# Scores by row halves of the array, one PSUM ring, one transposing DMA for q and k, masks on the vector engine

## The chip, the cores and the metric

The kernel runs on one core of one Trainium2 chip. A core has engines that run side by side: TensorE (matrix products, PE in the profile; its weight loads are PEld), VectorE (DVE), ScalarE (ACT), GpSimd (POOL) and SyncE (SP), and 16 DMA engines that they share. GpSimd and SyncE issue the transfers of this kernel. The metric is the device time of one execution in microseconds.

## The reference, cut to what matters

Four sequences of 768 positions with eight heads of 64: attention with a local window of 96 and eight global positions, a distance bias per head, then a two-layer network with a squared ReLU on all 3072 rows.

```python
scores = scale * np.matmul(q, k.transpose(0, 1, 3, 2))        # q, k, v: (4, 8, 768, 64)
rel = pos[:, None] - pos[None, :]
is_global = pos[None, :] < n_global                           # 8
is_local = (rel >= 0) & (rel < n_local)                       # 96
dist = np.where(is_global & ~is_local, float(n_local), np.abs(rel))
scores = scores - slopes[:, None, None] * dist                # one slope per head
scores = np.where(is_global | is_local, scores, -1e9)
a = softmax(scores)
x = np.matmul(a, v)                                           # then (3072, 512)
r = np.maximum(x @ w_in, 0.0)                                 # w_in (512, 2048)
out = (r * r) @ w_out                                         # w_out (2048, 512)
```

## The kernel before, in words

The 3072 rows are 24 tiles of 128; each sequence has six. A tile's queries look at the keys of their own tile and of the tile before (the eight global keys of the sequence are copied into columns of that one which the window doesn't reach). The first tile of a sequence has its own keys alone. Two tiles make a block of the network; there are 12 blocks, and w_in and w_out are cut into eight steps.

*A tile's way.* GpSimd loads q, k and v with a cast to bf16 (`swdge`, line 186; tile 0's q and k come from SyncE in fp32, line 194). For tiles below `JQK` = 10 TensorE transposes q and k (`emit_tr`, line 375), and ACT or DVE copies the transposes out (`any_copy`, lines 297 and 299). q goes to `qz`, where each pair of heads has two blocks of 128 rows: the first with the even head in rows 0 to 63 and zeros below, the second with the odd head in rows 64 to 127 and zeros above. From tile 10 on SyncE transposes with two DMAs (`emit_dT`, lines 414 and 418); q is then loaded by two DMAs into `qpad`, which holds the zeros already. One product of 128 rows by 256 columns gives the scores of two heads for one block of keys (`emit_sc`, line 442). A tile has eight of these, two in each of four PSUM tiles `sc`; the first tile of a sequence has four. ACT takes exp (line 482), DVE multiplies by the mask factors `E` (line 503). For tiles 0 to 2 (`NBIAS`) the mask is added on TensorE instead, by products of `sid` and `pb` (line 451). `po` (line 549) is the product with v, which has a column of ones per head for the sum; DVE divides (lines 574 and 575) to `x`. x is transposed by TensorE (line 611) for tiles below `JX` = 10 and by a SyncE DMA (line 635) from there on.

*The network.* For each block and step, `hT` (line 659) is eight products of 256 columns, ACT applies ReLU (line 680), DVE squares (line 692), and `acc` (line 723) takes four products of 512 columns, two per tile. After eight steps a tile's acc is copied out (297 or 299) and stored by SyncE (line 768).

*PSUM* has eight banks: two for acc, three shared by hT and the transposes, two for sc, one for po. q and k have ten load buffers each; v of all tiles has its own.

*Order.* `Plan` (lines 23 to 94) puts every operation on an engine: a list scheduler with hand-set costs, lags and landing times, which takes at each step the operation that can start first (then by `key`). The instructions of each engine run in this order; a wait holds up all that stands behind it. Scores of a tile run ahead of the block that needs them by about `LEAD` = 12 network steps, and its transposing DMAs wait for the transposed x of three tiles earlier.

*Start.* GpSimd makes the identity, issues q and k of tile 1, makes the position mask `pb` in four steps (lines 248 to 254), then issues v of tiles 0 and 1, tile 2 and so on, with the weights between the tiles (lines 277 to 285). DVE clears `qz` and writes all 24 columns of ones (line 243).

Of the kernel before, what the change touches and what calls it, by code (L numbers as in the profile page):

```python
# [22 lines left out]
class Plan:  # L23
# [7 lines left out]

    LAG = {"PE": 0.25, "ACT": 0.15, "DVE": 0.12, "SP": 2.6, "POOLQ": 2.5, "DMA": 0.0}

# [16 lines left out]
    def run(self):  # L50
        rings = {}
        free = {e: 0.0 for e in self.LAG}
# [10 lines left out]
        while ready:  # L63
            best = None
            for o in ready:
                at = o["at"]
                if o["takes"]:
                    tag, bufs, users = o["takes"]
                    ring = rings.setdefault(tag, [])
                    if len(ring) >= bufs:  # L70
                        old = ring[-bufs]
                        if any("end" not in u for u in old):
                            continue
                        at = max([at] + [self.after(u, o["engines"]) for u in old])
                for e, cost in o["engines"].items():
                    r = (max(at, free[e]), o["key"], cost, o["n"])
                    if best is None or r < best[0]:
                        best = (r, o, e)
# [3 lines left out]
            o["start"], o["engine"], o["end"] = r[0], e, r[0] + o["engines"][e]  # L82
            free[e] = o["end"]
            if o["takes"]:
                rings[o["takes"][0]].append(o["takes"][2])
# [12 lines left out]
def kernel(  # L98
# [32 lines left out]
    NG = NBLK * NSTEP  # L131
    NACC = 2
    NPLAIN = 1
    NFIRST = 4
    NBIAS = 3
    JQK, JX = 10, 10
    NQ, NPAD, NKT, NQZ = 10, 8, 2 * TPB, 4
# [4 lines left out]
    ps_h = ctx.enter_context(tc.tile_pool(name="ps_h", bufs=5 - NACC, space=PSUM))  # L142
    ps_sc = ctx.enter_context(tc.tile_pool(name="ps_sc", bufs=2, space=PSUM))
    ps_o = ctx.enter_context(tc.tile_pool(name="ps_o", bufs=1, space=PSUM))
# [5 lines left out]
    q_ring = [const([P, d_model], BF16, f"q_{i}") for i in range(NQ)]  # L150
    q_pad = [const([P, NPAIR, 2, P], BF16, f"qpad_{i}") for i in range(NPAD)]
    k_ring = [const([P, d_model], BF16, f"k_{i}") for i in range(NQ)]
    v_sb = [const([P, H, D + 1], BF16, f"v_{j}") for j in range(NT)]
    kT = [const([P, NPAIR, P], BF16, f"kT_{i}") for i in range(NKT)]
    qz = [const([P, NPAIR, 2, P], BF16, f"qz_{i}") for i in range(NQZ)]
# [4 lines left out]
    E = const([P, NPAIR, 2, 2, P], BF16, "E")  # L160
    E0 = const([P, NPAIR, 2, P], BF16, "E0")
# [4 lines left out]
    zero = const([P, 4 * P], BF16, "zero")  # L166
    plan = Plan()
    NHS = 14
    E_AT = 14.0
    NWARM = 8  # L170
    HOLD = {}
# [4 lines left out]
    clock = [4.2]  # L176
# [8 lines left out]
    def swdge(name, dst, src, t):  # L185
        nc.gpsimd.dma_start(out=dst, in_=src)  # L186
        clock[0] += t
        land[name] = clock[0]

    q_tile, k_tile = {}, {}  # L190
    for j in range(NPLAIN):
        for n, src in (("q", q), ("k", k)):
            t_ = const([P, d_model], FP32, f"plain_{n}{j}")
            nc.sync.dma_start(
                out=t_.rearrange("p (h d) -> p h d", h=H),
                in_=src_rows(src, j).rearrange("h p d -> p h d"),
            )
            (q_tile if n == "q" else k_tile)[j] = t_
            land[n, j] = 4.1 + 2.1 * j + (1.05 if n == "k" else 0.0)


    def load_v(j):
        swdge(("v", j), v_sb[j][:, :, :D], src_rows(v, j).rearrange("h p d -> p h d"), 0.85)

    def load_qk(j):
        k_tile[j] = k_ring[j % NQ]
        todo = [("k", k_tile[j], k)]
        if j < JQK:
            q_tile[j] = q_ring[j % NQ]
            todo.insert(0, ("q", q_tile[j], q))  # L210
        else:
            q_tile[j] = q_pad[j % NPAD]
            s_ = src_rows(q, j).rearrange("(a e) p d -> e p a d", e=2)
            for e in range(2):
                swdge(("q", j), q_tile[j][:, :, e, e * D : (e + 1) * D], s_[e], 0.43)
        for n, dst, src in todo:
            swdge(
                (n, j), dst.rearrange("p (h d) -> p h d", h=H),
                src_rows(src, j).rearrange("h p d -> p h d"), 0.85,
            )  # L220

    def load_tile(j):
        load_qk(j)
        load_v(j)
# [17 lines left out]
    for j in range(NT):  # L242
        nc.vector.memset(v_sb[j][:, :, D : D + 1], 1.0)
    make_identity(nc, ident)
    load_qk(1)


    nc.gpsimd.iota(pbi, pattern=[[-P, 2], [-1, P]], base=0, channel_multiplier=1)
    nc.gpsimd.tensor_copy(pb, pbi)
    nc.gpsimd.affine_select(  # L250
        out=pb, in_=pb, compare_op=Alu.is_ge, fill=MASK_VAL,
        base=0, pattern=[[P, 2], [1, P]], channel_multiplier=-1,
    )
    nc.gpsimd.affine_select(
        out=pb, in_=pb, compare_op=Alu.is_ge, fill=MASK_VAL,
        base=n_local - 1, pattern=[[-P, 2], [-1, P]], channel_multiplier=1,
    )
    load_v(0)
    load_v(1)
    nc.vector.tensor_copy(ident32, ident)  # L260
    nc.vector.memset(qz[0].bitcast(I32), 0)
    nc.vector.memset(qz[1].bitcast(I32), 0)
    for h in range(H):
        nc.vector.tensor_scalar_mul(sid[h], ident, float(slopes[h] / scale))
    nc.vector.tensor_copy(pb0, pb[:, 0, :])
    nc.vector.tensor_scalar_max(
        pb0[:n_global, :], pb0[:n_global, :], float(-n_local)
    )
    nc.vector.memset(pb[:n_global, 1, :], float(-n_local))
    nc.vector.memset(qz[2].bitcast(I32), 0)  # L270
    nc.vector.memset(qz[3].bitcast(I32), 0)

    warm = ps_o.tile([P, 4 * P], FP32, name="warm", tag="po")
    for i in range(NWARM):
        nc.tensor.matmul(out=warm, lhsT=zero[:, :P], rhs=zero, start=True, stop=True)

    load_tile(2)
    load_w_in(0)
    load_tile(3)
    load_w_out(0)  # L280
    for w in range(1, NSTEP):
        load_w_in(w)
        load_w_out(w)
        if w in (3, 5):
            load_tile(NFIRST + (w - 3) // 2)
# [9 lines left out]
    def any_copy(e, dst, src):  # L295
        if e == "ACT":
            nc.scalar.copy(dst, src)  # L297
        else:
# [4 lines left out]
            ("E", pair), {"ACT": 0.65}, key=0.3 + pair, ready=E_AT,  # L303
            emit=lambda e, pair=pair: [
                nc.scalar.activation(
                    E[:, pair, :, h, :], pb, Act.Exp, scale=float(slopes[2 * pair + h])
                )
                for h in range(2)
            ],
        )  # L310
        for pair in range(NPAIR)
    ]

    def emit_E0(e, c):

        pairs = slice(2 * c, 2 * c + 2)
        nc.vector.tensor_copy(E0[:, pairs], E[:, pairs, 0])
        nc.vector.tensor_max(
            E0[:n_global, pairs], E[:n_global, pairs, 0], E[:n_global, pairs, 1]
        )  # L320
# [3 lines left out]
            ("E0", c), {"DVE": 0.6}, emit=lambda e, c=c: emit_E0(e, c), key=4 + c,  # L324
            deps=maskE[2 * c : 2 * c + 2],
        )
        for c in range(2)
# [3 lines left out]
    qz_users = [[] for _ in range(NQZ)]  # L331
    kT_users = [[] for _ in range(NKT)]
    qk_users = [[] for _ in range(NQ)]
    pad_users = [[] for _ in range(NPAD)]
# [5 lines left out]
    for j in range(NT):  # L340
# [3 lines left out]
        base = need - LEAD + 4 * (j % 2)  # L344


        if j in late:
            def emit_load(e, j=j):
                if j == JQK:
                    for i in range(NPAD):  # L350
                        nc.gpsimd.memset(q_pad[i].bitcast(I32), 0)
                load_tile(j)
            ld = plan.op(
                ("load", j), {"POOLQ": 2.6}, emit_load,
                deps=qk_users[j % NQ] + (pad_users[j % NPAD] if j >= JQK else []),
                key=base, ready=clock[0],
            )
            qk_users[j % NQ] = []
            if j >= JQK:
                pad_users[j % NPAD] = []  # L360
# [3 lines left out]
        zi, ki = j % NQZ, j % NKT  # L364
        fp = j < NPLAIN
        parts = []
        for n in ("q", "k") if j < JQK else ():
            users = []

            def emit_tr(e, j=j, n=n, fp=fp):  # L370
                pool, tag = ps_h, "hT"
                tr = pool.tile([P, NPAIR, P], FP32 if fp else BF16, name=f"tr{n}", tag=tag)
                src = (q_tile if n == "q" else k_tile)[j]
# [8 lines left out]
                ("tr", n, j), {"PE": 0.85 if fp else 0.24}, emit_tr,  # L382
                deps=[land[n, j]], key=base, ready=HOLD.get(j, 0.0),
                takes=("hT", 5 - NACC, users),
            )
            users.append(tr)
            if n == "q":
                for e_ in range(2):
                    half = slice(e_ * D, (e_ + 1) * D)

                    def emit_z(e, j=j, e_=e_, half=half, zi=zi):
                        any_copy(e, qz[zi][half, :, e_, :], tiles["tr", "q", j][half])

                    z = plan.op(
                        ("z", e_, j), {"DVE": 0.7 if fp else 0.43, "ACT": 0.57}, emit_z,
                        deps=[tr] + qz_users[zi], key=base + 0.1,
                    )
                    users.append(z)
                    parts.append(z)
            else:  # L400
                def emit_T(e, j=j, n=n, ki=ki):
                    any_copy(e, kT[ki], tiles["tr", n, j])

                c = plan.op(
# [412 lines left out]
```

The softmax here doesn't subtract the row's maximum and nothing guards it: scores larger than these inputs give would overflow.

## Time and profile before

| What | Value |
|---|---|
| Median of 8 runs | 225.87 us (225.43 to 226.69) |
| The profiled execution | 225.98 us |
| Its span, first to last instruction | 224.2 us |
| TensorE busy | 212.0 us (95%) |
| VectorE / ScalarE busy | 145.8 (65%) / 123.3 (55%) |
| DMA queue of GpSimd (loads) | 79,424 packets, 13.38 MB |
| DMA queue of SyncE (stores, transposes) | 35,696 packets, 14.16 MB |
| Mean granted TensorE clock | 0.991 |

The page's second part cuts the span into 40 slices of 5.6 us; a digit is a busy share in tenths. A line of the timeline gives start, duration, engine, line, operation, out<-in, shapes and count, and in brackets the idle time before it with what ended it. A product's duration holds the depth of the array, so the distance between starts, and not the duration, is what a product takes from the stream. A DMA row of GpSimd or SyncE is the time of issuing; how long the transfer takes to land is given apart.

### The profile page before, as it was taken

Reading aid. Unit: us, or ns where it says so; the run is one execution under the profiler, and the core shown is the slowest. Engines: PE = TensorE matmul, PEld = TensorE weight load, DVE = VectorE, ACT = ScalarE, POOL = GpSimd, SP = SyncE. Lnnn points to the kernel's source line nnn. Section 1 sums busy time; section 2 is a strip of 40 time slices with the busy share of each in tenths; the row PEclk is TensorE's granted clock in tenths of the full one; section 3 lists DMA queues with packets and bytes.
Section 4 is the critical chain, followed back from the end, with each engine's and each line's share of the span. In section 5 each row is a group of like instructions: output and inputs, shape, how many; then the busy total and the mean of one; then the engine's idle time right before and its main releaser. Section 6 shows DMA issues by size and latency. Waiting matters only on the chain.

```text
span 224.2 us, 4803 instructions
## 1 busy us (share of the span) xinstructions
PE 212.0 (95%) x1817; PEld 152.5 (68%) x1848; DVE 145.8 (65%) x380; ACT 123.3 (55%) x225; POOL 88.1 (39%) x118
## 2 busy tenths in 40 slices
PE   7399899999999999999999999999999999999992
PEld 3388567765777777776767767776776776776750
DVE  6466858676766768666666766867656856844530
ACT  2459666673755945645544744744645645643530
POOL 8996687699988975323705000000000000000000
PEclk9969999999999999999999999999999999999999
DMA  9999999999999999999997984166724430300202
GB/s 128 106 155 200 182 196 181 173 177 147 150 169 152 144 163 160 118 231 119 129 216 102 121 134 95 34 156 95 150 41 96 126 69 18 117 8 20 94 0 94
DMA packets 115142, 27.83 MB, mean 124 GB/s; under 512 B 105776, under 2 KB 112176, under 8 KB 115120
## 3 DMA queue, kind: packets, MB, share of 16 engines
q0 software_dynamic: 79424, 13.38, 80.4%
q1 hardware_dynamic: 35696, 14.16, 32.0%
q8 instruction: 14, 0.23, 0.4%
q14 instruction: 8, 0.07, 0.1%
HBM read 27.26 MB, written 6.29 MB: 150 GB/s over the span
## 4 chain that ended last, share of the span: by engine, by line
PE 81%; POOL 6%; DMA 4%; DVE 4%; ACT 2%; issue 1%; POOLq 0%
PE acc L723 35%; PE hT L659 35%; PE sc L442 7%; PE po L549 4%; DMA win<-in_moe_w_in_dram 4%; DVE hs L692 2%; POOL q L186 1%; POOL v L186 1%; POOL k L186 1%; ACT hr L680 1%; DVE o L299 1%; POOL win L186 1%; PE trx L611 1%; POOL wout L186 1%; ACT qz L297 1%
## 5 line engine op out<-in xcount | busy, mean ns | idle before, releaser
L659 PE MATMUL hT<-xT,win 128*128 128x256 bf16 x768 | 98.6, 273 | 1.1 <-DMA win<-in_moe_w_in_dram 0.7
L680 ACT ACTIVATE hr<-hT 128x512 f32<-128x512 f32 x96 | 57.3, 597 | 75.3 <-PE hT L659 73.3
L723 PE MATMUL acc<-wout,hs 128*128 128x512 bf16 x353 | 94.8, 379 | 1.6
L659 PEld LDWEIGHTS <-win 128*128 128x128 bf16 x768 | 74.6, 98 | 24.3 <-DMA win<-in_moe_w_in_dram 1.6
L692 DVE TENSOR_TENSOR hs<-hr 128x512 bf16<-128x512 f32 x96 | 66.0, 687 | 26.0 <-ACT hr L680 24.6
L723 PEld LDWEIGHTS <-hs 128*128 128x128 bf16 x384 | 34.5, 98 | 22.8
L482 ACT ACTIVATE esc<-sc 128x512 bf16<-128x512 f32 x78 | 46.2, 592 | 2.4 <-PE sc L442 2.3
L442 PE MATMUL sc<-qz,kT 128*128 128x256 bf16 x176 | 35.4, 277 | 0.5 <-DVE kT L299 0.3
L503 DVE TENSOR_TENSOR at<-esc,E 128x512 bf16<-128x512 bf16 x78 | 32.4, 416 | 0.1
L186 POOL DMA_DIRECT2D qpad<-in_q_dram x28 | 21.6, 803 | 23.6 <-DMA qz<-qpad 23.6
L186 POOL DMA_DIRECT2D v<-in_v_dram x24 | 22.0, 915 | 2.9 <-DVE at L503 2.1
L186 POOL DMA_DIRECT2D k<-in_k_dram x23 | 21.1, 919 | 2.9 <-PE sc L442 1.5
L575 DVE TENSOR_TENSOR x<-po,rs 128x256 bf16<-128x256 f32 x48 | 20.4, 424 | 1.7
L549 PEld LDWEIGHTS <-at 128*128 128x128 bf16 x352 | 17.2, 99 | 5.9
L574 DVE RECIPROCAL rs<-po 128x4 f32<-128x4 f32 x48 | 8.6, 180 | 18.5 <-PE po L549 17.9
L442 PEld LDWEIGHTS <-kT 128*128 128x128 bf16 x176 | 17.1, 99 | 3.4 <-DVE kT L299 0.8
L549 PE MATMUL po<-v,at 128*128 128x65 bf16 x352 | 18.9, 195 | 0.0
L299 DVE COPY o<-acc 128x512 f32<-128x512 f32 (+1 forms) x12 | 7.9, 662 | 8.2 <-PE acc L723 4.3
L297 ACT COPY o<-acc 128x512 f32<-128x512 f32 (+1 forms) x13 | 7.4, 570 | 5.3 <-PE acc L723 5.2
L522 DVE COPY kT<-kT 128x32 bf16<-128x32 bf16 x16 | 3.6, 226 | 9.2 <-PE sc L442 9.2
L297 ACT COPY qz<-trq 64x512 bf16<-64x512 bf16 x10 | 5.8, 580 | 6.5 <-DVE qz L299 4.7
L186 POOL DMA_DIRECT2D q<-in_q_dram x9 | 8.4, 930 | 1.5 <-DMA wout<-in_moe_w_out_dram 1.2
(52 smaller groups left out, 92.3 us busy)
## 6 DMA issues: line engine op xcount, KB each, us to landing
out_dram<-o SPq DMA_DIRECT2D x23, 256.0 KB, 2.5
v<-in_v_dram POOLq DMA_DIRECT2D x24, 128.0 KB, 6.7
k<-in_k_dram POOLq DMA_DIRECT2D x23, 128.0 KB, 6.4
win<-in_moe_w_in_dram POOLq DMA_DIRECT2D x8, 256.0 KB, 8.6
wout<-in_moe_w_out_dram POOLq DMA_DIRECT2D x8, 256.0 KB, 8.8
qpad<-in_q_dram POOLq DMA_DIRECT2D x28, 64.0 KB, 4.8
q<-in_q_dram POOLq DMA_DIRECT2D x9, 128.0 KB, 7.7
plain_q<-in_q_dram SPq DMA_DIRECT2D x1, 256.0 KB, 3.2
```

The lines of the kernel that those rows point to most:

```text
L186: nc.gpsimd.dma_start(out=dst, in_=src)
L297: nc.scalar.copy(dst, src)
L299: nc.vector.tensor_copy(dst, src)
L442: nc.tensor.matmul(out=sc[:, i, :, :], lhsT=kT[kj % NKT][:, p_, :], rhs=qz[zi][:, p_, :, :], start=True, stop=j >= NBIAS, skip_group_check ...
L482: nc.scalar.activation(out=esc, in_=sc.rearrange("p a b c -> p (a b c)"), func=Act.Exp, scale=scale,)
L503: nc.vector.tensor_mul(at, tiles.pop(("esc", j, pair)), bias.rearrange("p a b c -> p (a b c)"))
L549: nc.tensor.matmul(out=po[:, hi, :], lhsT=at[:, pair % 2 if first else i, h % 2, :], rhs=v_sb[kj][:, h, :], start=(i == 0), stop=(i == len ...
L575: nc.vector.tensor_tensor(out=x[:, 4 * hf : 4 * hf + 4, :], in0=po[:, :, :D], in1=rs.to_broadcast([P, 4, D]), op=Alu.mult,)
L659: nc.tensor.matmul(out=hT[:, c, :], lhsT=w_in_sb[s][:, kt, c * P : (c + 1) * P], rhs=tiles["xT", blk][:, kt, :], start=(kt == 0), stop=(kt ...
L680: nc.scalar.activation(hr, tiles.pop(("hT", blk, s)), Act.Relu)
L692: nc.vector.tensor_mul(hs, hr, hr)
L723: nc.tensor.matmul(out=tiles["acc", blk, sub], lhsT=hs[:, c, sub * P : (sub + 1) * P], rhs=w_out_sb[s][:, c, :], start=(s == 0 and c == 0) ...
```

## The change

- **Scores.** q and k of a tile stand transposed side by side in one buffer `qkT`, 64 rows per head: even heads in rows 0 to 63, odd heads in rows 64 to 127. A score product takes 64 rows and 128 columns of one head, odd and even in turn, into different banks. A tile gives four banks of [128, 4 x 128] (two for a first tile), keyed by odd/even and by group; from tile 4 on all 16 products of a tile are one operation that takes four banks at once (`takes` may now hold several).
- **PSUM.** Two banks for acc, six in one ring `g` for everything else.
- **Transposes.** `JQK` = `JX` = 6. From tile 6 on one DMA transposes q and k together. No zeros and no `qpad`. Six load buffers in place of ten.
- **Masks.** GpSimd only makes the positions; identities and `pb` are made on DVE. The tables `E` and `E0` are laid out by odd/even.
- **Ones.** Six tiles' columns of ones at the start, the other 18 later in DVE's stream, ahead of the loads of those tiles.
- **Loads.** q of tile 1, the positions, k of tile 1, v of 0 and 1, then the first step of w_in ahead of tile 2, and a written order of tiles and weights.
- **Planner.** A pull of 0.05 per unit of `key` (`URGE`), start times of the engines, and other costs.
- ACT runs one exp on a junk element at the start.

```diff
@@ class Plan @@
+    URGE = 0.05
                 for e, cost in o["engines"].items():
-                    r = (max(at, free[e]), o["key"], cost, o["n"])
+                    start = max(at, free[e])
+                    r = (start + self.URGE * o["key"], start, cost, o["n"])
...
@@ pools and buffers @@
-    JQK, JX = 10, 10
-    NQ, NPAD, NKT, NQZ = 10, 8, 2 * TPB, 4
+    JQK, JX = 6, 6
+    NQ, NKT = 6, 2 * TPB
+    NG = 8 - NACC
+    G = ("g", NG)
...
-    ps_h = ctx.enter_context(tc.tile_pool(name="ps_h", bufs=5 - NACC, space=PSUM))
-    ps_sc = ctx.enter_context(tc.tile_pool(name="ps_sc", bufs=2, space=PSUM))
-    ps_o = ctx.enter_context(tc.tile_pool(name="ps_o", bufs=1, space=PSUM))
+    ps_g = ctx.enter_context(tc.tile_pool(name="ps_g", bufs=NG, space=PSUM))
...
@@ start @@
-    for j in range(NT):
+    for j in range(NFIRST + 2):
         nc.vector.memset(v_sb[j][:, :, D : D + 1], 1.0)
-    make_identity(nc, ident)
-    load_qk(1)
+    load_part(0, 1)
     nc.gpsimd.iota(pbi, pattern=[[-P, 2], [-1, P]], base=0, channel_multiplier=1)
-    nc.gpsimd.tensor_copy(pb, pbi)
-    nc.gpsimd.affine_select(...)
-    nc.gpsimd.affine_select(...)
+    load_part(1, 1)
     load_v(0)
     load_v(1)
+    nc.scalar.activation(junk, zero[:, :1], Act.Exp)
...
+    nc.vector.tensor_scalar(ident32, pbi[:, 0, :], 0.0, None, op0=Alu.is_equal)
+    nc.vector.tensor_scalar(ident, pbi[:, 0, :], 0.0, None, op0=Alu.is_equal)
+    nc.vector.scalar_tensor_tensor(
+        out=pbt, in0=pbi, scalar=MASK_VAL, in1=pbi, op0=Alu.mult, op1=Alu.min
+    )
+    nc.vector.tensor_scalar(
+        pbw, pbi, float(n_local - 1), -MASK_VAL, op0=Alu.add, op1=Alu.mult
+    )
+    nc.vector.tensor_tensor(out=pb, in0=pbt, in1=pbw, op=Alu.min)
...
+    for w in "i0 T2 i1 T3 i2 o0 i3 o1 i4 o2 T4 i5 o3 i6 o4 T5 i7 o5 o6 o7".split():
+        kind, n = w[0], int(w[1:])
+        {"T": load_tile, "i": load_w_in, "o": load_w_out}[kind](n)
...
@@ tile loop @@
-                nc.sync.dma_start_transpose(
-                    out=qz[zi].rearrange("p a b c -> p (a b) c"),
-                    in_=q_tile[j].rearrange("p a b c -> p (a b c)"),
-                )
-                nc.sync.dma_start_transpose(out=kT[ki], in_=k_tile[j])
+                nc.sync.dma_start_transpose(
+                    out=T_.rearrange("p n a c -> p (n a) c"),
+                    in_=qk_ring[j % NQ].rearrange("p n c -> p (n c)"),
+                )
...
-                sc = ps_sc.tile([P, 2, 2, P], FP32, name="sc", tag="sc")
-                for i in range(2):
-                    p_, kj = (pair + i, j) if first else (pair, j - i)
-                    nc.tensor.matmul(
-                        out=sc[:, i, :, :],
-                        lhsT=kT[kj % NKT][:, p_, :],
-                        rhs=qz[zi][:, p_, :, :],
+            for g in gs:
+                for odd in range(2):
+                    sc[odd, g] = ps_g.tile([P, 4, P], FP32, name="sc", tag="g")
...
+            for g, pair, at, kt in todo:
+                for odd in range(2):
+                    half = slice(odd * D, (odd + 1) * D)
+                    nc.tensor.matmul(
+                        out=sc[odd, g][:, at, :],
+                        lhsT=qkT[(j - kt) % NKT][half, 1, pair, :],
+                        rhs=qkT[j % NKT][half, 0, pair, :],
...
+        for gs in [(0,), (1,)] if j < NSPLIT and not first else [tuple(range(groups))]:
+            n = 8 * len(gs)
+            o = plan.op(
+                ("sc", j, gs[0]), {"PE": 0.25 + 0.029 * n + (0.056 * n if j < NBIAS else 0)},
+                lambda e, gs=gs, f=emit_sc: f(e, gs), deps=deps, key=base + 1 + 2 * gs[0],
+                takes=(*G, busers[2 * gs[0] : 2 * gs[-1] + 2]),
+            )
```

## The prediction

> **What bounds the kernel now.** I read the page's busy rows first, then the TensorE timeline, then the SyncE and GpSimd issue timelines with the DMA landings. Row 2 of the page:
>
> ```profile
> PE   7399899999999999999999999999999999999992
> PEclk9969999999999999999999999999999999999999
> DMA  9999999999999999999997984166724430300202
> ```
>
> From the sixth slice (28 us) on TensorE is full; what it lacks is lost in the first slices, where the clock also drops once. The DMA engines are full up to slice 22 (123 us). So two stages have two limits: up to about 30 us loads arrive too late, after that the length of TensorE's stream decides. The stream's pitches come from starts in the timeline:
>
> ```profile
> 8.40 0.27 PE L451 MATMUL sc<-pb,sid 128*128 128x128 bf16 x2
> 11.26 0.40 PE L375 MATMUL trq<-ident,q 128*128 128x128 bf16 x4 [2.58 <-DMA q<-in_q_dram]
> ...
> 112.50 0.41 PE L549 MATMUL po<-v,at 128*128 128x65 bf16 x8
> 112.74 1.03 PE L723 MATMUL acc<-wout,hs 128*128 128x512 bf16 x4
> 113.60 1.04 PE L659 MATMUL hT<-xT,win 128*128 128x256 bf16 x8
> 114.48 0.38 PE L442 MATMUL sc<-qz,kT 128*128 128x256 bf16 x2
> 114.70 1.03 PE L723 MATMUL acc<-wout,hs 128*128 128x512 bf16 x3
> ```
>
> Start to start: eight po take 0.24 (0.030 each), four acc 0.86 (0.216), eight hT 0.88 (0.1094), two sc 0.22 (0.109). A four-block transpose takes 0.23, a 128-column bias product 0.055 (two in 0.11 at 8 us). The sum over the program: hT 768 x 0.1094 = 84.0, acc 384 x 0.216 = 83.1, sc 176 x 0.109 = 19.2, bias 2.2, po 352 x 0.030 = 10.6, transposes 7.6; 206.7 us. TensorE's first transpose starts at 4.6, its last acc ends at 219.6: 8.3 us of idle, nearly all before 31 us (2.58 of it in the line above, and 12.1 to 15.3 at half clock). Then 4.6 to the span's end at 224.2 (eviction, store), and 1.8 to the execution's own 225.98; the median of eight runs, 225.87, is 0.1 less, so I use the execution's frame as it is.
>
> **The change part by part.**
>
> *Row-halved scores.* 176 products of 256 columns on all 128 rows (half of them zeros) become 352 of 128 columns on 64 rows, odd and even heads in different banks. If both halves of the array work at once, a tile of 16 takes eight pairs at 0.055 to 0.060 (the bias pitch; or two po, each with a weight load of its own, at 0.030): 0.46, against 8 x 0.109 = 0.875 now. Here a rule speaks against it. The Trainium skill, "TensorEngine Tiling (Array Packing)", Key Properties, says that changing the tiling mode drains TensorE, and each score group now stands between full-array work, so two changes a group. No row shows a drain; the nearest is the pipeline's depth: an sc of 0.109 pitch lasts 0.277 in row 5, so 0.17 until it is out. Two of these make a tile of 16 cost 0.46 + 0.34 = 0.80, and one of 8 0.57 instead of 0.437. On the other side the same skill, "TensorE: Matmul & The Clock Gate", Part 3, has row tiles start 4 ns apart and names no such cost; by it alone 0.46 and 0.23. A drain should partly hide under the next weight loads, so I take 0.25 a group: 0.71 and 0.48. For all 24 tiles: 17 later non-first tiles save 0.165 each (2.8), tiles 1 to 3, cut into two groups, lose 0.085 each, four first tiles lose 0.04 each: 2.4 us net; 9.1 by the side-by-side rule alone, 0.2 with the full drain.
>
> *Transposes of tiles 6 to 9 leave TensorE.* q, k and x of four tiles: 12 x 0.23 = 2.7 us off the full stream. 22 evictions to ACT and DVE go as well; both have cover (55% and 65% busy), so that is nothing. In place of them SyncE issues transposing DMAs from tile 6 on; qz and kT become one of the size of qz.
>
> *When tile 6 is ready.* This replaces TensorE work in the stage where DMA is full, so I follow it. Loads go out in order on GpSimd:
>
> ```profile
> 1.44 1.04 POOL L186 DMA_DIRECT2D q<-in_q_dram  x1
> 2.47 0.88 POOL L186 DMA_DIRECT2D k<-in_k_dram  x1
> 3.35 0.38 POOL L248 IOTA pbi<- 128x256 int32 x1
> ...
> 5.11 1.78 POOL L186 DMA_DIRECT2D v<-in_v_dram  x2
> ...
> 36.52 0.88 POOL L186 DMA_DIRECT2D k<-in_k_dram  x1
> ```
>
> The last is k of tile 6, landed 8.3 us later, at 44.8. The identity (0.7 ahead of the first load) and three of four mask steps leave this queue: the first v starts at 0.75 + 1.04 + 0.44 + 0.88 = 3.1 instead of 5.1. What follows moves the same bytes, so tile 6 lands at 42.8. Then its transpose:
>
> ```profile
> 60.21 2.28 SPq L414 DMA_TRANSPOSE qz<-qpad  x1
> ...
> 93.52 1.19 SPq L635 DMA_TRANSPOSE xT<-x  x1
> ```
>
> The first took 8.5 us, with 512 KB of stores ahead of it on SyncE's queue; the second, half as large, with nothing ahead and loads filling DMA, 4.5, where such an xT takes 2.4 without loads. qz without loads takes 3.1 at best; 3.1 x 4.5 / 2.4 = 5.8, about 6. Tile 6 has no store ahead of it: ready at 42.9 + 6.0 = 48.9. Bounds: 3.1 and 11.0 (the longest qz). A rule would give less: the Trainium skill, "DMA: Bandwidth & Descriptors", Latency and other measured facts, has 261 GB/s for transposing DMAs, so 1.0 us for 256 KB after an issue of 2.3, ready at 46.2. The traced ones all took longer, and I keep the row.
>
> Ahead of tile 6's scores TensorE's list has 104 hT (11.4), 48 acc (10.4), 88 scores (7 groups of 8 and 2 of 16: 4.8), 40 bias (2.2), 88 po (2.7), 72 transposes (4.9): 36.4 us. From 4.6 with the idle of the first stage cut from 8 to 5 (tile 1's scores no longer stand behind q of tile 2, and the first win comes before it), it gets there at 46. So it waits 2.9 us there, in order, and everything behind it too: relu, exp, the acc of other blocks. If the transpose takes 3.1 this wait is gone (-2.9); at 11.0 it is 5 us longer.
>
> *Behind tile 6* the list has 664 hT (72.6), 336 acc (72.7), 3 groups of 8 and 15 of 16 (12.1), 264 po (8.0): 165.4 us.
>
> *Waits added.* (a) One score group takes four of six banks at once. The latest of these is freed by a relu of an hT that ended 2.8 us before (po, hT and eight acc stand between); drain and relu take 0.9. Nothing, and up to 0.3 a tile (4.5 in all) if ACT falls behind. (b) po follows its scores after hT, acc, hT and the second half, 2.95 us; two exp (0.59 each), a mul (0.42) and handovers come to 2.1. Nothing. (c) Six load buffers: the load of tile j waits for the transpose of tile j-6, some 49 us earlier than its own; a load lands in 4 to 9 us. GpSimd's 23.6 us of waits for pads in the profile of before were as harmless. (d) Later transposes stand behind stores and xT on SyncE, one instruction fewer per tile than now; tile 9's waits for xT of tile 6 and is ready some 6 us before its scores.
>
> *Masks on DVE, V ones first.* DVE drops four memsets (0.49 each) and defers 18 of 24 ones (0.04 each); it gains two identities and three mask steps, which the trace doesn't show on it; 128x256 rows of DVE take 0.27 to 0.42, so about 2 us with the identities, then eight sid (1.2) and pb0 (0.9): done near 6.2, while the first scores wait for two evictions on ACT until 7.1. Hidden by 0.9; any excess falls into the wait for tile 6. The deferred ones (18 x 0.04) gate only loads from tile 6 on, which GpSimd reaches after 30 us. The early exp on ACT fetches its table (1.3 us) while ACT is idle.
>
> **Sum.** 48.9 + 165.4 + 0.8 (small idle behind it; now about as much) + 4.6 = 219.7 span, + 1.8 = 221.5 us, 2.0% under before.
>
> **Rivals.**
> *R1, nothing waits and halves overlap fully.* Tile 6 at 46, groups at 0.46 and 0.23: 221.5 - 2.9 - 18 x 0.25 = 214.1; with either alone 217 to 218.6. For it: po's pitch shows weight loads that hide. Against: DMA rows of 8 to 11 us.
> *R2, slower: the halves don't run side by side.* Each 64-row product then takes a turn of its own, 16 x 0.055 + 0.34 = 1.22 a tile and 0.78 a group of 8: + 15 x 0.51 + 3 x 0.30 = 8.6, 230.1 us. Then the change does not do what it says. It turns slower than before from 0.71 + 4.4/18 = 0.95 us for 16. Nothing in the profile shows two products at once, which speaks for it; that the operands lie on separate rows and banks speaks against.
> *R3, transposes in the full stage come late:* 11.0 instead of 6, tile 6 at 53.9: + 5.0, 226.5 us; a gap of 2.58 also went before the half clock.
> *R4, gain and wait cancel,* 225.5 to 226.3.
>
> **How the numbers follow.** Forecast 0.50, its own range 218.5 to 223.5; R1 and its halves 0.23; R2 0.13; R3 0.10; R4 0.04. The predicted time is 221.5. The range leaves out the far end of R1 and R2: 215.5 to 227. Differences under 0.2% can't be told from no change here. Faster: 0.50 + 0.23 + a fifth of R3 = 0.75; same 0.04; slower 0.21.
>
> **What would show it.** In the timeline, 16 scores from first start to the next product at 0.71 (0.46 R1, 0.80 with the full drain, 1.2 R2), odd and even starting together; a TensorE wait at tile 6's scores near 46 to 49 us released by the transposing DMA; after it, slices at 9 and a block of two tiles in 16.3 us instead of 16.6; no transposes on TensorE after tile 5. The forecast falls if the groups of 16 take over 0.95, if the wait at tile 6 is over 7 us, or if waits for PSUM banks appear in each tile.

## The result

The changed kernel takes 224.27 us (median of 12 runs, 223.49 to 225.54) against 226.01 us before (33 runs). The ratio is 0.9931, 95% interval 0.9914 to 0.9948: 0.7% faster, about a third of the 2.0% forecast. The profiled execution took 224.18 us with a span of 222.4 us; the forecast had 221.5 and 219.7.

The page's second part of the changed kernel, 40 slices of 5.6 us:

```profile
PE   7889899947999999999999999999999999999992
PEclk9999999996999999999999999999999999999999
DMA  9999999999999999999959999432630810310201
```

Before, the lowest digit (3) stood in the second slice and the clock's one drop in the third. Now the second slice has 8, and there is a new hole in slices 9 and 10 (44.5 to 55.6 us), with a drop of the clock in the second of these. DMA is full there, as it was before.

TensorE's timeline of the changed kernel, at that hole and, further down, at a later group of scores (start, duration, engine, line, operation; in brackets the idle time and what ended it):

```profile
46.23 0.81 PE L716 MATMUL acc<-wout,hs 128*128 128x512 bf16 x3
51.35 0.61 PE L428 MATMUL sc<-qkT 64*128 64x128 bf16 x8 [4.31 <-DMA qkT<-qk]
51.89 1.89 PE L652 MATMUL hT<-xT,win 128*128 128x256 bf16 x8
53.57 1.56 PE L716 MATMUL acc<-wout,hs 128*128 128x512 bf16 x4
54.97 1.04 PE L652 MATMUL hT<-xT,win 128*128 128x256 bf16 x8
...
108.08 1.03 PE L716 MATMUL acc<-wout,hs 128*128 128x512 bf16 x4
109.04 0.23 PE L428 MATMUL sc<-qkT 64*128 64x128 bf16 x2
109.10 0.22 PE L428 MATMUL sc<-qkT,qkT 64*128 64x128 bf16 x2
...
109.44 0.22 PE L428 MATMUL sc<-qkT,qkT 64*128 64x128 bf16 x2
109.59 0.61 PE L652 MATMUL hT<-xT,win 128*128 128x256 bf16 x4
```

The wait is where the prediction put it: at tile 6's scores, ended by the transposing DMA. TensorE got there at about 46.9 (the three acc of 46.23 take 0.65). Behind the wait the same eight hT take 1.68 start to start, and 0.87 three microseconds later: the clock was at half.

The lower part shows the halves at work. Each row is two products, one of an even and one of an odd head, that start together; the next pair follows 0.057 later. From the first pair to the hT behind it is 0.55. Ahead of it the four acc take 0.96 instead of the usual 0.87, so a group of 16 costs 0.64 in all.

SyncE's issues of the changed kernel, and GpSimd's (start, time of issuing):

```profile
43.14 5.18 SPq L394 DMA_TRANSPOSE qkT<-qk  x2
```

```profile
34.80 0.88 POOL L189 DMA_DIRECT2D qk<-in_k_dram  x1
```

k of tile 6 landed 8.3 us after its issue, at 43.1 (forecast 42.8). The first transpose in SyncE's row is tile 6's. It landed 8.2 us after 43.14; the forecast had 6.0 for it. What the DMA engines did from 43 to 47 us, from the same trace (queue, packets, MB, time of the packets as a share of 16 engines' time; over 100% where several packets overlap on an engine):

```profile
q0 software_dynamic: 4866, 0.61, 240.9%
q1 hardware_dynamic: 26, 0.01, 1.0%
```

The first queue holds GpSimd's loads, the second SyncE's transfers. Nearly nothing of the transpose had moved: loads that GpSimd had issued ahead, nearly all for tiles 7 and later, kept the engines full. That these loads are the reason is shown further down, by the run that holds them back.

The table of stretches shows the price (us of span; length, busy us of TensorE, weight loads, VectorE, ScalarE, GpSimd with their instructions, then clock, DMA share, GB/s):

```profile
46.00:58.00 12.00, 7.63 (x55) 4.70 (x55) 3.50 (x8) 2.88 (x5) 6.44 (x8) 0.86 2.05 175
58.00:215.00 157.00, 154.79 (x1439) 106.74 (x1465) 108.76 (x249) 86.22 (x155) 30.68 (x35) 1.00 0.99 109
```

In twelve microseconds TensorE is without work for 4.4, and the mean clock is 0.86. A clock of one half for 3.41 us (51.2 to 54.65) makes that mean and loses 1.7 us. Afterwards TensorE is full at full clock.

### The profile page after: what moved, and what is told of

It reads as the page before. It is cut to its first block, busy times and chain, and to the rows that moved or that the text cites. A ratio compares the mean times of both kernels' runs of the same rounds, so it can differ in the third digit from the quotient of the medians.

```text
span 222.4 us, 4977 instructions
## 1 busy us (share of the span) xinstructions
PE 207.0 (93%) x1944; PEld 141.3 (64%) x1976; DVE 143.5 (65%) x369; ACT 117.9 (53%) x215; POOL 73.9 (33%) x91
## 4 chain that ended last, share of the span: by engine, by line
PE 69%; DMA 19%; POOL 6%; DVE 2%; issue 2%; ACT 1%; POOLq 0%; SPq 0%
PE hT L652 32%; PE acc L716 30%; DMA win<-in_moe_w_in_dram 4%; PE sc L428 4%; DMA wout<-in_moe_w_out_dram 4%; DMA qk<-in_k_dram 4%; DMA qkT<-qk 4%; DMA xT<-x 3%; PE po L541 3%; POOL qk L189 3%; POOL v L189 2%; POOL win L189 1%; DVE hs L685 1%; POOL wout L189 1%; ACT hr L673 1%
## 5 line engine op out<-in xcount | busy, mean ns | idle before, releaser
L716 PE MATMUL acc<-wout,hs 128*128 128x512 bf16 x352 | 91.1, 381 | 2.5 <-DVE hs L685 0.6
L652 PEld LDWEIGHTS <-win 128*128 128x128 bf16 x768 | 71.1, 98 | 18.4 <-DMA win<-in_moe_w_in_dram 1.4
L474 ACT ACTIVATE esc<-sc 128x512 bf16<-128x512 f32 x78 | 42.3, 597 | 21.2 <-PE sc L428 21.2
L189 POOL DMA_DIRECT2D qk<-in_q_dram x23 | 20.7, 898 | 47.9 <-DMA qkT<-qk 44.2
L189 POOL DMA_DIRECT2D qk<-in_k_dram x23 | 20.5, 893 | 6.6 <-DMA v<-in_v_dram 5.8
L428 PEld LDWEIGHTS <-qkT 64*128 64x128 bf16 x352 | 10.0, 95 | 14.9 <-issue 7.8
L428 PE MATMUL sc<-qkT 64*128 64x128 bf16 x192 | 13.5, 223 | 5.6 <-DMA qkT<-qk 4.3
L300 ACT COPY o<-acc 128x512 f32<-128x512 f32 (+1 forms) x13 | 7.4, 571 | 10.2 <-PE acc L716 9.5
L428 PE MATMUL sc<-qkT,qkT 64*128 64x128 bf16 x160 | 11.4, 216 | 0.0
L515 DVE COPY qkT<-qkT 128x32 bf16<-128x32 bf16 x16 | 3.7, 230 | 7.0 <-PE sc L428 7.0
L474 ACT ACTIVATE at<-sc 128x512 bf16<-128x512 f32 x10 | 5.4, 594 | 3.1 <-PE sc L438 3.0
```

Source lines behind the costliest of these rows:

```text
L428: nc.tensor.matmul(out=sc[odd, g][:, at, :], lhsT=qkT[(j - kt) % NKT][half, 1, pair, :], rhs=qkT[j % NKT][half, 0, pair, :], start=True, s ...
L474: nc.scalar.activation(out=esc, in_=tiles.pop(("sc", j, odd, g)).rearrange("p a c -> p (a c)"), func=Act.Exp, scale=scale,)
L652: nc.tensor.matmul(out=hT[:, c, :], lhsT=w_in_sb[s][:, kt, c * P : (c + 1) * P], rhs=tiles["xT", blk][:, kt, :], start=(kt == 0), stop=(kt ...
L716: nc.tensor.matmul(out=tiles["acc", blk, sub], lhsT=hs[:, c, sub * P : (sub + 1) * P], rhs=w_out_sb[s][:, c, :], start=(s == 0 and c == 0) ...
```

## The experiments

Theory A: the gain was lost at tile 6. Loads that run ahead fill the DMA engines, its transpose lands late, TensorE waits 4.3 us in order, and the wait brings 1.7 us of half clock; all other parts of the change do what they should, with a price of about 0.19 us for each group of row-half scores between full-array products, where a group is the scores that TensorE takes in one go, 16 products or 8. The rivals put the loss elsewhere: into the groups themselves (halves that don't really run together, or costlier changes of mode), or into the 18 transposing DMAs as a burden on the whole stream. In the recorded expectations A stands for this theory; what a rival expects is told beside it. All ratios are to the kernel before, with 95% intervals.

### Tiles 6 and 7 transposed by TensorE (e1_tr67)

```diff
-    JQK, JX = 6, 6
+    JQK, JX = 8, 6
```

> The changed kernel with q and k of tiles 6 and 7 transposed by TensorE again (JQK 8; x still by DMA from tile 6). Theory A (the wait of 4.3 us at tile 6's scores and the half clock behind it, about 1.7 us, are what the forecast lacked): both go, 0.9 us of transposes (16 x 0.057) come back, 224.3 - 4.3 - 1.7 + 0.9 = 219.2 us, and no TensorE wait over 1 us between 30 and 200 us. Theory B (DMA stays the limit in this stage, the wait only moves to tile 8's scores or to xT): 222 to 225 us with a new wait released by a DMA between 50 and 75 us.

Measured: 220.40 us, ratio 0.9764 (0.9724 to 0.9805), span 218.7. TensorE's timeline of this run:

```profile
48.04 0.59 PE L716 MATMUL acc<-wout,hs 128*128 128x512 bf16 x2
48.56 0.40 PE L428 MATMUL sc<-qkT 64*128 64x128 bf16 x8
48.90 1.05 PE L652 MATMUL hT<-xT,win 128*128 128x256 bf16 x8
```

and its table of stretches:

```profile
46.00:58.00 12.00, 11.90 (x117) 7.96 (x117) 6.74 (x17) 5.69 (x11) 9.05 (x12) 1.00 2.11 179
58.00:215.00 157.00, 154.24 (x1416) 105.47 (x1440) 107.00 (x244) 85.25 (x153) 27.98 (x32) 1.00 0.89 107
```

No wait, no half clock: 11.90 busy of 12 in place of 7.63. TensorE carries four more transposes than in the changed kernel (0.92 us) and the whole is still 3.7 us shorter by the spans. The scores of tile 6 start 2.8 us earlier and the half clock's 1.7 are gone, which makes 4.5; two of the four extra transposes (0.46) and a wait of 0.34 for an x stand behind tile 6 and bring it to 3.7. With everything else of the change in place, groups and 16 transposing DMAs included, the gain is 2.4%, so the rivals can't hold the loss. A's sum had 219.2: it left out that TensorE's transposes wait for loads, 3.6 us in this run against 1.0 in the changed kernel.

### The wait filled with products of zeros (e2_fill)

```diff
+            if j == 6:
+                for _ in range(18):
+                    nc.tensor.matmul(
+                        out=sc[0, 0].rearrange("p a c -> p (a c)"), lhsT=zero[:, :P], rhs=zero,
+                        start=True, stop=True,
+                    )
```

> The changed kernel with 18 products of zeros (128 x 512, written to the bank that tile 6's scores overwrite) issued just ahead of tile 6's scores, so that TensorE works through 3.9 us of the wait. The wait for the transposing DMA stays. Theory A (the idle wait itself brings the half clock that follows): the clock stays whole after 51 us, 224.3 - 1.7 = 222.6 us. Theory B (the half clock has another cause, or costs nothing since other waits absorb it): 224.3 us, within 0.5.

Measured: 223.06 us, ratio 0.9874 (0.9828 to 0.992).

```profile
47.38 4.05 PE L427 MATMUL sc<-zero 128*128 128x512 bf16 x18
51.85 0.40 PE L434 MATMUL sc<-qkT 64*128 64x128 bf16 x8 [0.42 <-DMA qkT<-qk]
52.18 1.05 PE L658 MATMUL hT<-xT,win 128*128 128x256 bf16 x8
```

The transpose is as late as before (scores at 51.85), but TensorE was busy until 0.42 us ahead of it, and the hT behind it last 1.05 instead of 1.89: no half clock. Useless work made the kernel 0.6% faster, 1.3 us by the two ratios against the 1.7 worked out from the clock. From tile 6's scores to the last group of acc this profile has 161.3 us (51.85 to 213.18), and the changed kernel's has 162.9 (51.35 to 214.27): 1.6 less. So the half clock is a term of its own, set off by the idle time and not by the lateness. This profile has another half clock, of 3.41 us from 14.5 us on, behind several waits of at most 1.4 us; the three other runs have a mean clock of 0.999 or more.

### Everything but the moved transposes (e5_j10)

```diff
-    JQK, JX = 6, 6
+    JQK, JX = 10, 10
```

> The changed kernel with the transposes of q, k and x of tiles 6 to 9 on TensorE as in the kernel before (JQK and JX 10): everything of the change but the transposes moved to DMA in the full stage. Theory A (moving them saves 2.7 us of stream and costs a wait of 4.3 and a half clock of 1.7): 224.3 - 6.0 + 2.7 = 221.0 us. If the second tile pair (8, 9) by DMA costs nothing more, this is 1.8 us above the run with tiles 6 and 7 alone on TensorE. Theory B (transposing DMAs for tiles 8 and 9 cost hidden time too): under 220 us.

Measured: 222.36 us, ratio 0.9845 (0.9823 to 0.9868), span 220.5. Without the moved transposes the change brings 1.55%. The changed kernel, which takes 2.7 us more off TensorE, is 1.9 us slower than this. Against the first experiment the eight groups of transposes between them (q and k of tiles 8 and 9, x of 6 to 9) are 8 x 0.23 = 1.8 us, and the ratios of the two runs differ by 1.8: moving these is worth all that it takes off the stream. A's 221.0 was 1.4 too low. TensorE's transposes wait 4.1 us for loads in this run, against 1.0 in the changed kernel, which may be what that sum lacks.

### Each later tile's scores in two groups (e6_split)

```diff
-    NSPLIT = 4
+    NSPLIT = 24
```

> The changed kernel with the scores of every later tile cut into two groups of 8 as tiles 1 to 3 have them (NSPLIT 24): the same products, one more change between full and half rows in and out for each of 17 tiles. Theory A (a change in and out costs time, read from the trace as about 0.09 ahead of a group and 0.10 behind it): + 17 x 0.19 = 3.2 us, 227.5 us, slots of 0.33 for 8 with 0.09 lost ahead of them. Theory B (no cost of changing): 224.3 us within 0.5, slots of 0.23 for 8.

Measured: 228.15 us, ratio 1.0105 (1.0065 to 1.0145), 3.9 us over the changed kernel.

```profile
51.18 0.40 PE L428 MATMUL sc<-qkT 64*128 64x128 bf16 x8 [3.67 <-DMA qkT<-qk]
...
108.88 0.81 PE L716 MATMUL acc<-wout,hs 128*128 128x512 bf16 x3
109.62 0.23 PE L428 MATMUL sc<-qkT 64*128 64x128 bf16 x2
...
109.80 0.22 PE L428 MATMUL sc<-qkT,qkT 64*128 64x128 bf16 x2
109.95 1.05 PE L652 MATMUL hT<-xT,win 128*128 128x256 bf16 x8
...
216.98 4.06 PE L716 MATMUL acc<-wout,hs 128*128 128x512 bf16 x18 [0.55 <-DVE hs L685]
```

The last line is the last group of acc; in the changed kernel it is this one:

```profile
214.27 4.06 PE L716 MATMUL acc<-wout,hs 128*128 128x512 bf16 x17 [0.55 <-DVE hs L685]
```

Four pairs take 4 x 0.057 = 0.23, but it is 0.33 to the hT behind them: 0.10 lost. Ahead, three acc take 0.74 instead of 0.65: 0.09. So each group costs 0.19 beyond its pairs, and 17 more groups 3.2 us; 3.9 was measured by the ratios, 2.7 by the profiled spans (225.1 against 222.4). The profile says where the difference comes from: two of the 17 stand ahead of the wait at tile 6's scores, which is 3.7 us here instead of 4.3. From these scores to the last acc it is 165.8 us here and 162.9 in the changed kernel, 2.9 for the other 15, and 15 x 0.19 is 2.9. This sizes the rule of the Trainium skill, "TensorEngine Tiling (Array Packing)", Key Properties, that a change of tiling mode drains TensorE: not nothing, not 0.34, but 0.19 for the way in and out, if the whole price is that drain, which no run here separates.

### All even heads first, then all odd (e4_apart)

```diff
-            for g, pair, at, kt in todo:
-                for odd in range(2):
+            for odd in range(2):
+                for g, pair, at, kt in todo:
```

> The changed kernel with the score products of a group ordered all even heads first, then all odd heads, in place of alternating; the same products and banks. Theory A (alternating halves run at the same time, a pair in 0.058): apart they take turns, 16 in 0.9 to 1.1 in place of 0.55 us, + 18 groups x about 0.4 less the eight-groups' half: + 7 us, 231 us. Theory B (64-row products are simply as fast alone as in pairs, by weight loads and not by overlap): no change, 224.3 us.

Measured: 228.51 us, ratio 1.012 (1.0079 to 1.0161), 4.3 us over the changed kernel, not 7.

```profile
111.36 0.23 PE L428 MATMUL sc<-qkT 64*128 64x128 bf16 x1
...
111.53 0.22 PE L428 MATMUL sc<-qkT,qkT 64*128 64x128 bf16 x1
111.59 0.23 PE L428 MATMUL sc<-qkT 64*128 64x128 bf16 x2
...
111.76 0.24 PE L428 MATMUL sc<-qkT,qkT 64*128 64x128 bf16 x2
111.83 0.22 PE L428 MATMUL sc<-qkT 64*128 64x128 bf16 x1
...
112.15 1.05 PE L652 MATMUL hT<-xT,win 128*128 128x256 bf16 x8
```

The last column holds the count: four slots with one product, four with two, four with one, each about 0.057. A 64-row product alone takes as long as a pair; that is what running side by side is worth. I had expected 16 slots. TensorE started odd products beside even ones that stand four places ahead in program order, so 12 slots were enough, 0.79 in place of 0.55. A group of 8 lost nothing (0.34 us to the hT behind it, 0.33 in the changed kernel): its four odd products start beside its four even ones. From tile 6's scores to the last acc the profile has 167.85 us (51.15 to 219.00) in place of 162.92, 4.9 more. The 15 groups of 16 in between account for 3.6 of this by 0.24 each. Another 1.0 is lost ahead of tile 7's scores, where the half clock lasted 6.8 us after the same wait of 4.31, and 0.3 is left. The two groups of 16 ahead of the wait cost nothing, since it takes them up.

### Two load buffers (e3_nq2)

```diff
-    NQ, NKT = 6, 2 * TPB
+    NQ, NKT = 2, 2 * TPB
```

This was meant to hold back the loads behind tile 7, but it also leaves the true scores of tiles 1 to 3 out: the loads of tiles 1 to 5 are issued ahead of the loop, so with two buffers q and k of tiles 1 to 3 are overwritten, and their scores come from the data of tiles 4 and 5.

> The changed kernel with two load buffers for q and k in place of six: the load of tile 8 then waits until tile 6's transpose has landed, so loads no longer fill the DMA engines while tiles 6 and 7 are transposed. TensorE's order is the same. Theory A (the loads running ahead stretch the transpose of tile 6 to 8.2 us): it lands in 4 to 6 us, the wait at tile 6's scores shrinks by 2.5 to 4 us, with the half clock 219 to 222 us. Theory B (issue and own transfer take the 8 us): 224.3 us. Theory C (two buffers make loads late in every later tile): over 226 us with waits at scores throughout.

Measured: 244.07 us, ratio 1.081 (1.0762 to 1.0858). TensorE stood 28.4 us at the start, until the load of tile 5 landed at 34.3, and worked at half clock around it. That is a stall of the experiment's own making, and it decides nothing about tile 6. The next experiment asks the same question without it.

### Loads behind tile 6's transpose (e7_gate)

GpSimd reads a column of tile 6's transposed q before it issues the load of tile 7, so all later loads stand behind the transpose.

```diff
+                if j == 7:
+                    nc.gpsimd.tensor_copy(gate, qkT[6][:, 0, 0, :1])
...
-                ("load", j), {"POOLQ": 2.6}, emit_load, deps=qk_users[j % NQ] + [ones[j]],
+                ("load", j), {"POOLQ": 2.6}, emit_load, deps=qk_users[j % NQ] + [ones[j]] + T6,
...
+            T6 = T6 or [T]
```

> The changed kernel where GpSimd reads one column of tile 6's transposed q before it issues the load of tile 7, so that this and all later loads start after tile 6's transpose has landed. TensorE's and SyncE's orders are the same. Theory A (loads that run ahead stretch that transpose from about 4 to 8.2 us): it lands 4 to 5 us after its issue at about 43, near 47.5, the wait at tile 6's scores shrinks from 4.3 to under 1 us and the half clock behind it goes: 218.5 to 219.5 us, or up to 221 if tile 7's late load makes tile 7's scores wait. Theory B (the 8 us are the transpose's own): 224.3 us and a wait of 4 us as before.

Measured: 225.24 us, ratio 0.9974 (0.9936 to 1.0012). The DMA queues of this run in the same four microseconds as above:

```profile
q1 hardware_dynamic: 1056, 0.26, 33.9%
q0 software_dynamic: 55, 0.01, 2.7%
```

1056 packets of the transpose in place of 26. It was issued at 42.97 and landed in 3.2 us in place of 8.2. TensorE's timeline of this run:

```profile
46.10 0.81 PE L721 MATMUL acc<-wout,hs 128*128 128x512 bf16 x3
46.85 0.40 PE L433 MATMUL sc<-qkT 64*128 64x128 bf16 x8
...
53.52 1.03 PE L721 MATMUL acc<-wout,hs 128*128 128x512 bf16 x4
58.64 0.28 PE L433 MATMUL sc<-qkT 64*128 64x128 bf16 x2 [4.09 <-DMA qkT<-qk]
```

Tile 6's scores start at 46.85 with no wait. The loads are what made the transpose late. But tile 7's load now came late, its transpose took 6.6 us among the loads, and the wait and a half clock (6.8 us long this time) moved to tile 7. So the time is about the changed kernel's (the intervals overlap) and not A's 218.5 to 221. The cause is shown; as a cure it only shifts the wait.

### Tile 6 loaded ahead of the last weights (e8_early6)

```diff
-    NFIRST = 4
+    NFIRST = 5
-    for w in "i0 T2 i1 T3 i2 o0 i3 o1 i4 o2 T4 i5 o3 i6 o4 T5 i7 o5 o6 o7".split():
+    for w in "i0 T2 i1 T3 i2 o0 i3 o1 i4 o2 T4 i5 o3 i6 o4 T5 i7 T6 o5 o6 o7".split():
```

> The changed kernel with tile 6's load ahead of the last three steps of w_out instead of behind them (tile 6 joins the written load order). Theory A (tile 6 is late because it stands behind 1.3 us a weight step in a full DMA): its k lands 3.9 us earlier, near 39, the transpose near 47.3, a wait of 0 to 1.5 us without half clock, 219 to 221 us. Theory B (the wait moves to acc, whose w_out steps now land later, or the transpose lands no earlier): 223 to 225 us with waits of acc for w_out.

Measured: 228.27 us, ratio 1.0126 (1.0094 to 1.0158). SyncE's issues of this run; its first transposes are these:

```profile
45.83 5.15 SPq L394 DMA_TRANSPOSE qkT<-qk  x2
```

k of tile 6 landed at 39.3, 3.8 us earlier, as meant, yet nothing was transposed before 45.8. The planner had put tile 7's transpose ahead of tile 6's in SyncE's order; it waited for tile 7's k, and tile 6's stood behind it and landed at 57. TensorE waited 7.4 us at tile 6's scores, and the half clock lasted 10.2 us. Neither theory had this. An earlier load is worth nothing when the queue behind it is in the wrong order.

### The same, with the transposes in order (e9_early6t)

```diff
-    NFIRST = 4
+    NFIRST = 5
...
-    for w in "i0 T2 i1 T3 i2 o0 i3 o1 i4 o2 T4 i5 o3 i6 o4 T5 i7 o5 o6 o7".split():
+    for w in "i0 T2 i1 T3 i2 o0 i3 o1 i4 o2 T4 i5 o3 i6 o4 T5 i7 T6 o5 o6 o7".split():
...
-                ("T", j), {"SP": 2.0}, emit_dT,
-                deps=[land["q", j], land["k", j], xT_op[j - 3]] + ku, key=base - 6,
+                ("T", j), {"SP": 4.0 if j < 8 else 2.0}, emit_dT,
+                deps=[land["q", j], land["k", j], xT_op[j - 3]] + ku + last_T, key=base - 6,
...
+            last_T = [T]
```

> As the run with tile 6's load ahead of the last three steps of w_out, but with tile 6's transpose issued before tile 7's (there it stood behind tile 7's on SyncE and waited for tile 7's k), and the planner told that these two take 4 us. Theory A (the whole loss is tile 6's transpose being late): k of tile 6 lands at 39.3, the transpose, still among loads, 8 us later at 47.5, TensorE comes to its scores at about 49 and does not wait, no half clock: 224.3 - 4.3 - 1.7 = 218.3 us, up to 220 if tile 7's scores wait a little. Theory B (w_out's later steps make acc wait instead, or tile 7 waits): 222 us or more.

Measured: 220.82 us, ratio 0.9782 (0.9763 to 0.9801), span 217.9, the shortest of all profiled executions.

```profile
39.19 1.33 SPq L394 DMA_TRANSPOSE qkT<-qk  x1
...
47.20 1.24 SPq L394 DMA_TRANSPOSE qkT<-qk  x1
```

Tile 6's transpose is issued at 39.19 and takes 7.5 us, hardly less than in the changed kernel, but it is there at 46.7, and tile 6's scores start at 49.55 with no wait. What is left, among this run's waits (engine, waiting work, line, what it waited for: us, times, longest):

```profile
PE sc L429 <- DMA qkT<-qk: 0.5, 1, 0.5
```

is 0.5 us at tile 7; hT waits 0.9 us more, in two places, for a transposed x. This is the changed kernel with all of its parts and none of its transposes back on TensorE, and it beats both kernels: 1.5% under the changed one. A had 218.3 to 220 and B 222 or more, so A is nearer, and the wait and the half clock are gone as it says.

### Tile 6 alone transposed by TensorE (e10_tr6)

```diff
-    JQK, JX = 6, 6
+    JQK, JX = 7, 6
```

> The changed kernel with q and k of tile 6 alone transposed by TensorE (JQK 7), tile 7 by DMA. Against tiles 6 and 7 on TensorE it saves 8 transposes, 0.45 us. Theory A (tile 7's transpose, first on SyncE now, lands by 54 to 55, its scores come at about 57): no wait, 219.9 us by the ratio of that run less 0.45. Theory B (in the full stage tile 7's transpose is late in its turn): a wait at tile 7's scores, 221.5 us or more.

Measured: 221.49 us, ratio 0.9813 (0.9788 to 0.9838). There is no wait at tile 7's scores, so it isn't B, but it is 1.6 us over A's 219.9; hT waits 1.2 us in two places for a transposed x, which may be why it isn't shorter than the first experiment's 220.40 (the intervals overlap). One tile kept on TensorE is enough to remove the stall.

## Why the prediction was right or wrong

The direction was right and the time lies in the range, but the size was 2.0% against 0.7% measured. The step that failed is tile 6: its transposing DMA was put at 6.0 us and took 8.2, and the half clock behind the wait was put at nothing and cost 1.7 us. That the time still lies in the range is partly luck, since 1.2 us of this came back from score groups that were taken too dear. By the prediction's own steps:

- **Scores by halves: right, somewhat too dear.** 0.71 was taken for 16, 0.64 measured; 0.48 for 8, 0.42 measured. Over 15 groups of 16 and 3 of 8 behind tile 6 that is 1.2 us less than forecast. R2 falls: pairs start together in the timeline, and a product alone costs as much as a pair. R1's 0.46 for the pairs alone was right, but the changes of mode come on top. (The 0.2 us net given for the full drain should be nothing, by the prediction's own 0.80 and 0.57; no later term rests on it.)
- **Transposes off TensorE: right in kind.** There are none after tile 5. The two runs that differ by eight of them are apart by 1.8 us, 0.23 a piece.
- **When tile 6 is ready: the load right, the transpose mis-sized.** Its k landed at 43.1 (forecast 42.8) and TensorE reached its scores at 46.9 (forecast 46). The transposing DMA was taken at 6.0, scaled from an xT in thinner traffic (packets of the loads took 168% of the engines' time in the 4.5 us from its issue, 241% beside tile 6's transpose); 8.2 was measured, and tiles 7 to 11 took 8.6 to 10.2. The scores started at 51.35, not 48.9: + 2.45 us. The row of 8.5, put down to the stores ahead of it, was nearer than the scaled one. The estimate that the prediction made from 261 GB/s (the Trainium skill, "DMA: Bandwidth & Descriptors", Latency and other measured facts), 1.0 + 2.3 us, fits the case without loads: there the whole took 3.2 us. Beside the loads it is off by a factor of 2.5.
- **The half clock: left out of the sum.** The prediction mentioned it beside R3, with a gap of 2.58 before, and gave it no price at its own wait of 2.9. It cost 1.7 us (3.41 us at half); the run with zeros gives 1.6. The Trainium skill, "TensorE: Matmul & The Clock Gate", Part 1, has the clock drop after at least one idle window of about 3.4 us and come back after a busy one of about the same length. This case's lengths agree: every half clock ahead of the last product lasts 3.41 us or a whole multiple of it in every kept trace. The condition doesn't: the gap of 2.58 before brought one too, and three runs (evens first, loads held back, tile 6 loaded early) dropped the clock 2.8 to 2.9 us after TensorE had stopped.
- **Behind tile 6, waits added, masks: right.** 219.7 + 2.45 + 1.7 - 1.2 = 222.65 against the measured span of 222.4. No wait of TensorE for a PSUM bank came back from tile to tile, the six load buffers held GpSimd for 44.2 us without harm, and the first scores started at 7.17 (7.1 in the forecast).
- **The rivals.** R3's mechanism is what happened, at 8.2 between the 6 taken and its 11, with the clock on top. The 0.10 for it was too low, since DMA rows of 8 to 11 us were in view. R1, with no wait, is nearly what the run with tile 6 loaded early gives: 220.8, where R1's one-sided cases had 217 to 218.6.

What stays open is why waits of nearly one length bring half clocks of different lengths. The changed kernel does so by itself: of its 13 runs, the profiled one among them, eight have a mean clock of 0.990 to 0.992 (median 223.96 us) and five 0.984 or 0.985 (median 225.25), about what one and two stretches of 3.41 us make of the mean. In the early stage, where TensorE waits for loads, a half clock costs nothing that shows: the kernel before has one in its profile (12.1 to 15.5 us), but its runs with a mean clock of 1.000 are no shorter than those with 0.984 to 0.992 (226.20 us against 225.49, medians of 9 and 12 runs taken beside the experiments). The effect of the new start alone was not measured apart from the scores.

## What to carry to other kernels

When work goes from the engine that is the bound to a DMA, ask first where its first result is needed: one tile at the seam (the first one that the DMA transposes), in the stage where DMA is full, ate two thirds of the gain here. Take the duration of a transfer from rows that run beside the same traffic (7 to 10 us here, 3 without), and where TensorE is the limit give a wait of several us (3.7 to 7.4 here) a second price for the clock behind it. What helped here was to leave the first tiles at the seam where they were, or to load the first one earlier and keep the queue that serves them in their order.

## What was not expected of the hardware

- TensorE ran row-half products out of program order: with all evens issued ahead of all odds, eight of 16 products shared a slot, the odd ones up to four places early.
- A lone product of 64 rows by 128 columns takes the same 0.057 as two on different halves.
- 18 products of zeros, 4.05 us of work for nothing, made the kernel 1.3 us faster, because the clock stayed at full behind them.
- With the loads held back, the moved wait of 4.09 us brought a half clock of 6.8 us instead of 3.41, so two waits of nearly equal length can differ twofold in the half clock behind them. With evens ahead of odds it was 6.8 us after the very same wait of 4.31.
